# Moving one batch's q and k transposes from TensorE to the DMA queue in a fused attention and MLP kernel

## The chip, the cores and the metric

The kernel runs on one core of a Trainium2 chip. The metric is the device time of one execution in microseconds. Executions of one kernel on one chip mostly agree within 0.3%. "Fast" and "slow" are the states that each run was given: slow is a run more than 1.5% above the fastest of the same kernel.

## The reference, cut to what matters

```python
def _attn_ref(q, k, v):                      # 8 batches, 8 heads, 576 positions, 64 wide
    scores = np.matmul(q, k.transpose(0, 1, 3, 2)) / np.sqrt(D)
    mask = np.abs(pos[:, None] - pos[None, :]) <= 32
    ...softmax over the masked scores...
    return np.matmul(attn, v)

def _moe_ref(x, w_in, w_out):                # x: 4608 x 512, w_in: 512 x 2048
    h = x @ w_in
    g = np.where(h > 0.0, h, np.exp(np.minimum(h, 0.0)) - 1.0)
    return g @ w_out
```

A narrow band of attention feeds two large matrix products. The products are most of the work of TensorE; the attention is threaded between them.

## The kernel before

The loop has 144 steps. A step has eight matmuls `ps` (x times w_in), four `psY` (g times w_out, two steps behind), and in three places, "dve", "mid" and "end", whatever a table has put there: casts, transposes, scores, loads. A quiet step takes 1.735 us, eight steps with their attention 15.32 us.

```python
for kk in range(NSTEP + LAG):
    run(kk, "first")
    if 1 <= kk < NSTEP:
        elu(kk - 1)
    run(kk, "dve")
    if kk < NSTEP:
        mm1(kk)                  # ps
    run(kk, "mid")
    ...mm2(kk - LAG)...          # psY
    run(kk, "end")
```

Attention goes by pairs of blocks of 64 queries. Pair 9 is the first to need batch 2's q and k, pair 13 batch 3's (step 37), pair 18 batch 4's (step 58). Scores need q and k with the 64 channels on the partitions, so each batch's q and k are transposed, in one of two ways:

```python
# On TensorE (batches 0 to 2): cast, transpose against the identity, evict from PSUM
at(19 + n, "mid", cast_qk, b, which, WHOLE, j0, 9, nc.vector)
at(20 + n, "mid", transpose_qk, b, which, WHOLE, j0, 9, nc.scalar, "s")

# By DMA (batches 3 to 7): cast, write the rows to DRAM, transpose on the way back
def write_rows(b, which):                        # issued by ScalarE
    nc.scalar.dma_start(out=..., in_=qk_b.pop((b, which, 0))...)

def transpose_rows(b, which):                    # issued by SyncE's queue
    nc.sync.dma_start_transpose(
        out=keys_or_queries(b, which), in_=in_dram.pop((b, which)))

def x_dma(i):                                    # from pair 10 on; the same queue
    nc.sync.dma_start_transpose(out=xT_of(i), in_=x_st...)
```

The transpose waits for the rows to have landed. SyncE's queue also carries the loads of q and k, and the output. v is loaded by GpSimd in short rows; VectorE copies it from `Ve` to `Vo` a few steps later. A "gate" is a DMA of one element that waits for a tile: what stands behind it in the queue can't start earlier.

```python
for m in range(3, VS):
    load_v(1, m)                                                 # batch 1's last v
gate(w_out_sb[0:1, NFO // 4 - 1, D_MODEL - 1:D_MODEL])
for which in range(2):
    load_qk(1, which, HALF_A)
gate(w_in_at(3))                                                 # w_in's fourth quarter
for which in range(2):
    load_qk(1, which, HALF_B)
for which in range(2):
    load_qk(2, which, WHOLE)
```

The softmax here doesn't subtract the row's maximum and nothing guards it: scores larger than these inputs give would overflow.

## Time and profile before

| | before |
|---|---|
| median of 3 runs | 309.51 us (309.19 to 310.4) |
| span of the profiled run | 307.9 us |
| TensorE busy | 95% of the span |
| share of TensorE in the chain that ended last | 81% |

The lines of the profile that carry this are in the prediction below: TensorE is full from 31 us to the tail, so the steps can be followed by the starts of their `ps` groups. All step starts below are such starts in the profiled run, in us from the beginning of the span.

### The profile page before, as it was taken

Reading aid. Unit: us, or ns where it says so; the run is one execution under the profiler, and the core shown is the slowest. Engines: PE = TensorE matmul, PEld = TensorE weight load, DVE = VectorE, ACT = ScalarE, POOL = GpSimd, SP = SyncE. Lnnn points to the kernel's source line nnn. Section 1 sums busy time; section 2 is a strip of 40 time slices with the busy share of each in tenths; the row PEclk is TensorE's granted clock in tenths of the full one; section 3 lists DMA queues with packets and bytes.
Section 4 is the critical chain, followed back from the end, with each engine's and each line's share of the span. In section 5 each row is a group of like instructions: output and inputs, shape, how many; then the busy total and the mean of one; then the engine's idle time right before and its main releaser. Section 6 shows DMA issues by size and latency. Waiting matters only on the chain.

```text
span 307.9 us, 7525 instructions
## 1 busy us (share of the span) xinstructions
PE 291.5 (95%) x3009; PEld 196.9 (64%) x3062; DVE 245.8 (80%) x478; ACT 169.4 (55%) x254; POOL 45.8 (15%) x64
## 2 busy tenths in 40 slices
PE   6778999999999999999999999999999999999994
PEld 2546666676666666666666666666666666666662
DVE  6776688899978788888887888888888787876663
ACT  3635656787664674767376737673636363634331
POOL 8841100952220302020202010000000000000000
PEclk9799999999999999999999999999999999999999
DMA  9999999999999899799999998377111111111011
GB/s 188 190 193 273 188 257 387 302 191 223 293 166 195 289 255 206 170 165 331 156 140 197 322 261 183 111 178 159 70 36 68 36 70 35 70 34 70 0 70 68
DMA packets 91654, 52.33 MB, mean 170 GB/s; under 512 B 76516, under 2 KB 81124, under 8 KB 91620
## 3 DMA queue, kind: packets, MB, share of 16 engines
q1 hardware_dynamic: 47444, 35.60, 47.4%
q0 software_dynamic: 42304, 9.51, 40.1%
q10 hardware_dynamic: 1872, 6.75, 5.8%
q8 instruction: 24, 0.39, 0.5%
q14 instruction: 10, 0.08, 0.1%
HBM read 36.70 MB, written 15.34 MB: 169 GB/s over the span
## 4 chain that ended last, share of the span: by engine, by line
PE 81%; DVE 7%; DMA 4%; POOL 3%; issue 2%; ACT 1%; DVEq 0%; POOLq 0%
PE ps L582 38%; PE psY L616 36%; DMA w_in_sb<-in_moe_w_in_dram 4%; PE psS L328 3%; PE psS L296 3%; DVE g_sb L601 2%; POOL Ve L141 1%; PE ptx L271 1%; DVE m_sb L591 1%; DVE x_st L340 1%; DVE pm L316 1%; ACT e_sb L589 1%; POOL c L135 1%; DVE y_sb L228 1%; PE psXT L349 1%
## 5 line engine op out<-in xcount | busy, mean ns | idle before, releaser
L589 ACT ACTIVATE e_sb<-ps 128x512 f32<-128x512 f32 (+1 forms) x145 | 86.2, 595 | 123.0 <-PE ps L582 115.4
L582 PE MATMUL ps<-xT,w_in_sb 128*128 128x256 bf16 x1152 | 149.3, 273 | 2.7 <-DVE m_sb L591 0.9
L616 PE MATMUL psY<-w_out_sb,g_sb 128*128 128x512 bf16 x525 | 139.1, 379 | 4.2 <-DMA w_out_sb<-in_moe_w_out_dram 0.9
L582 PEld LDWEIGHTS <-w_in_sb 128*128 128x128 bf16 x1152 | 110.7, 98 | 41.0 <-issue 2.3
L601 DVE SCALAR_TENSOR_TENSOR g_sb<-ps,m_sb 128x512 bf16<-128x512 f32 (+1 forms) x145 | 99.5, 686 | 13.1 <-PE ps L582 0.5
L591 DVE TENSOR_SCALAR m_sb<-e_sb 128x512 bf16<-128x512 f32 (+1 forms) x145 | 62.2, 429 | 35.3 <-ACT e_sb L589 33.3
L616 PEld LDWEIGHTS <-g_sb 128*128 128x128 bf16 x576 | 54.5, 98 | 39.9 <-DVE g_sb L601 1.6
L141 POOL DMA_DIRECT2D Ve<-in_v_dram x40 | 35.0, 885 | 130.7 <-PE psS L328 93.6
L307 ACT ACTIVATE pu<-psS 128x1024 bf16<-128x1024 f32 x36 | 36.6, 1019 | 1.9 <-PE psS L296 1.9
L340 DVE TENSOR_TENSOR x_st<-psS,rc 128x512 bf16<-128x512 f32 x36 | 24.9, 692 | 2.3 <-DMA xT<-x_st 1.1
L316 DVE TENSOR_TENSOR pm<-pu,masks 128x1024 bf16<-128x1024 bf16 x36 | 24.6, 683 | 1.4 <-ACT pu L307 1.3
L226 ACT CAST qkb<-f 128x768 bf16<-128x768 f32 (+1 forms) x30 | 25.4, 848 | 0.0
L328 PEld LDWEIGHTS <-pm 128*64 128x64 bf16 x576 | 11.2, 110 | 9.7 <-DVE pm L316 6.7
L152 DVE COPY Vo<-Ve 64x1040 bf16<-64x1040 bf16 x32 | 13.8, 431 | 1.4 <-DMA Ve<-in_v_dram 0.4
L328 PE MATMUL psS<-Ve,pm 128*64 128x65 bf16 x320 | 13.8, 196 | 0.5 <-DVE pm L316 0.3
L296 PEld LDWEIGHTS <-kT 64*128 64x128 bf16 x576 | 10.0, 97 | 5.3 <-issue 4.2
L228 DVE COPY y_sb<-psY 128x512 f32<-128x512 f32 x18 | 12.3, 686 | 1.0 <-PE psY L616 0.9
L296 PE MATMUL psS<-qT,kT 64*128 64x64 bf16 x576 | 12.4, 193 | 0.5 <-DVE kT L228 0.5
L328 PE MATMUL psS<-Vo,pm 128*64 128x65 bf16 x256 | 12.4, 196 | 0.2 <-DVE pm L316 0.2
L226 ACT COPY y_sb<-psY 128x512 f32<-128x512 f32 x18 | 10.5, 583 | 2.2 <-PE psY L616 2.2
L226 ACT COPY qT<-ptx 128x1152 bf16<-128x1152 bf16 (+2 forms) x8 | 7.5, 971 | 3.1 <-PE ptx L271 2.4
L271 PE MATMUL ptx<-ident,qkb 128*128 128x128 bf16 x90 | 7.1, 223 | 2.0 <-DVE qkb L228 1.9
(35 smaller groups left out, 68.3 us busy)
## 6 DMA issues: line engine op xcount, KB each, us to landing
out_dram<-y_sb SPq DMA_DIRECT2D x35, 256.0 KB, 2.8
f<-in_q_dram SPq DMA_DIRECT2D x12, 576.0 KB, 8.4
f<-in_k_dram SPq DMA_DIRECT2D x12, 576.0 KB, 9.2
in_dram<-qkb ACTq DMA_DIRECT2D x10, 576.0 KB, 7.3
Ve<-in_v_dram POOLq DMA_DIRECT2D x24, 128.0 KB, 10.3
w_in_sb<-in_moe_w_in_dram POOLq DMA_DIRECT2D x4, 512.0 KB, 14.0
w_out_sb<-in_moe_w_out_dram POOLq DMA_DIRECT2D x4, 512.0 KB, 16.6
Ve<-in_v_dram POOLq DMA_DIRECT2D x16, 96.0 KB, 9.5
```

Of the source, the lines that this page charges most:

```text
L141: nc.gpsimd.dma_start(out=V_e[b % 3][p0:p1, m, :, 0:D], in_=v[b, :, lo + p0:lo + p1, :].rearrange("h p d -> p h d"))
L226: nc.scalar.copy(d_, s_)
L296: nc.tensor.matmul(psS[:, h % 2, hp * 128 + z * QB:hp * 128 + (z + 1) * QB], lhsT=kT[b % 2][base:base + 64, KPAD + hp * S + QB * qb - WIN: ...
L307: nc.scalar.activation(pu, _bap(psS, [psS.ap[0], [1, 1024]]), AX.Exp, scale=SCALE)
L316: nc.vector.tensor_mul(pm, pu, _bap(mm, [mm.ap[0], [0, H], [1, 2 * QB]]))
L328: nc.tensor.matmul(psS[QB * z:QB * (z + 1), par, hp * VD:(hp + 1) * VD], lhsT=pm[:, par * HP + hp, z * QB:(z + 1) * QB], rhs=vv[:, qb // 2 ...
L340: nc.vector.tensor_mul(x_st, _bap(psS, [psS.ap[0], [VD, HP], [512, 2], [1, D]]), _bap(rc, [rc.ap[0], [2, HP], [1, 2], [0, D]]))
L582: nc.tensor.matmul(ps[:, j, :], lhsT=w_in_sb[:, do, fo * 128:(fo + 1) * 128], rhs=xT[t][:, :, do, :], start=(do == 0), stop=(do == NDO - 1))
L589: nc.scalar.activation(e_sb, ps, AX.Exp)
L591: nc.vector.tensor_scalar(m_sb, e_sb, -1.0, None, ALU.add)
L601: nc.vector.scalar_tensor_tensor(g_t[kk][:, z * w:(z + 1) * w, :], ps, 0.0, m_t[kk][z], ALU.max, ALU.min)
L616: nc.tensor.matmul(psY[t][ts], lhsT=g_sb[:, j, ts * 128:(ts + 1) * 128], rhs=w_out_sb[:, s * FG + j, :], start=(s == 0 and j == 0), stop=( ...
```

## The change

The intent: take batch 2's 36 transposes (four groups of nine) off TensorE, which is the bound, and send its q and k the way of batches 3 to 7. To make room, batch 1's second half and batch 2 are loaded earlier (behind w_out's third quarter instead of w_in's fourth), batch 3's loads wait for batch 2's last cast of k, batch 4's come later, and pairs 8 to 11 begin two steps later. Cut to its core:

```diff
-    gate(w_in_at(3))
+    gate(w_out_sb[0:1, 3 * NFO // 4 - 1, D_MODEL - 1:D_MODEL])
     for which in range(2):
         load_qk(1, which, HALF_B)
-    for which in range(2):
+    for which in (1, 0):
         load_qk(2, which, WHOLE)
...          (batch 1's first cast of k: from step 8's "dve" to step 7's "end")
-    begin = {4: 9, 5: 12, 6: 17, 7: 19, 8: 25, 10: 30, 12: 37}
+    begin = {4: 9, 5: 12, 6: 17, 7: 19, 8: 27, 10: 32, 12: 37}
...          (pair 9's transpose of x on TensorE: from its step's "end" to "mid")
-        l_qk, l_v, c0 = {2: (0, 0, 0), 3: (15, 24, 22)}.get(
-            b, (max(k0 - 36, 24), k0 - 22, k0 - 22))
+        l_qk, l_v, c0 = {2: (0, 0, 0), 3: (18, 24, 22)}.get(
+            b, (k0 - 28, k0 - 22, k0 - 22))
+        if b == 3:
+            at(22, "dve", hold_v, 3)
...
         if b == 2:
-            for n, (which, j0) in enumerate(((0, 0), (0, 9), (1, 0), (1, 9))):
-                at(19 + n, "mid", cast_qk, b, which, WHOLE, j0, 9, nc.vector)
-                at(20 + n, "mid", transpose_qk, b, which, WHOLE, j0, 9,
-                   nc.scalar, "s")
-            continue
+            when = [(15, "end", nc.scalar), (16, "dve", nc.vector),
+                    (18, "mid", nc.scalar), (18, "end", nc.scalar),
+                    (20, "mid", nc.scalar), (20, "end", nc.scalar)]
...          (a gate on the last cast of k, at step 18)
+                at({18: 20, 20: 23}[kk] if b == 2 else
+                   kk + (3 if kk == 29 else 4), "mid",
                    transpose_rows, b, which)
```

`l_qk`, `l_v` and `c0` are the steps at which a batch's loads of q and k, its loads of v and its casts begin.

More of the change, by code (lines that the diff above doesn't have):

```diff
@@ L491 @@
         for which in range(2):
-            at(*((kq + which, "dve") if kq == 7 else (kq - 1 + which, "mid")),
-               cast_qk, 1, which, part, 0, SJ // 2,
+            at(*((kq, ("dve", "end")[which]) if kq == 7 else
+                 (kq - 1 + which, "mid")), cast_qk, 1, which, part, 0, SJ // 2,
                (nc.scalar, nc.vector)[which])
@@ L521 @@
         if i < FIRST_DMA:
-            at(n, "end", x_transpose, i)
-            at(n, "end", x_evac, i, nc.scalar)
+            slot = "mid" if i == FIRST_DMA - 1 else "end"
+            at(n, slot, x_transpose, i)
+            at(n, slot, x_evac, i, nc.scalar)
         else:
@@ L530 @@
         k0 = begin[first_pair(b)]
-        l_qk, l_v, c0 = {2: (0, 0, 0), 3: (15, 24, 22)}.get(
-            b, (max(k0 - 36, 24), k0 - 22, k0 - 22))
+        l_qk, l_v, c0 = {2: (0, 0, 0), 3: (18, 24, 22)}.get(
+            b, (k0 - 28, k0 - 22, k0 - 22))
+        if b == 3:
+            at(22, "dve", hold_v, 3)
         if b >= 3:
-            at(l_qk, "mid", load_qk, b, 0, WHOLE)
-            at(l_qk + 1, "mid", load_qk, b, 1, WHOLE)
+            at(l_qk, "end", load_qk, b, 0, WHOLE)
+            at(l_qk + (b > 3), "end", load_qk, b, 1, WHOLE)
             for m in range(VS):
                 at(l_v + m, "mid", load_v, b, m)
-        for n, back in enumerate((3, 2, 1, 0) if b == 2 else (10, 8, 3, 2)):
+        for n, back in enumerate({2: (3, 2, 1, 0), 3: (6, 5, 3, 2)}.get(
+                b, (10, 8, 3, 2))):
             m0 = 2 * (n // 2)
@@ L542 @@
         if b == 2:
-            for n, (which, j0) in enumerate(((0, 0), (0, 9), (1, 0), (1, 9))):
-                at(19 + n, "mid", cast_qk, b, which, WHOLE, j0, 9, nc.vector)
-                at(20 + n, "mid", transpose_qk, b, which, WHOLE, j0, 9,
-                   nc.scalar, "s")
-            continue
-        free = [f for f in range(c0, k0) if f not in starts]
-        for n, (which, j0) in enumerate(
-                (which, j0) for which in range(2) for j0 in (0, 6, 12)):
-            at(free[n], "end", cast_qk, b, which, WHOLE, j0, 6,
-               nc.vector if free[n] < 24 else nc.scalar)
-            if j0 == 12:
-                at(free[n], "end", write_rows, b, which)
-                at(free[n] + (3 if free[n] == 29 else 4), "mid",
+            when = [(15, "end", nc.scalar), (16, "dve", nc.vector),
+                    (18, "mid", nc.scalar), (18, "end", nc.scalar),
+                    (20, "mid", nc.scalar), (20, "end", nc.scalar)]
+        else:
+            when = [(f, "end", nc.vector if f < 24 else nc.scalar)
+                    for f in range(c0, k0) if f not in starts]
+        for n in range(6):
+            which, j0 = (n // 3 + (b == 2)) % 2, 6 * (n % 3)
+            kk, slot, eng = when[n]
+            at(kk, slot, cast_qk, b, which, WHOLE, j0, 6, eng)
+            if j0 == 12:
+                if b == 2 and which == 1:
+                    at(kk, slot, lambda: gate(
+                        qk_b[2, 1, 0][0:1, SJ - 1, 0:1]))
+                at(kk, slot, write_rows, b, which)
+                at({18: 20, 20: 23}[kk] if b == 2 else
+                   kk + (3 if kk == 29 else 4), "mid",
                    transpose_rows, b, which)
```

## The prediction

> **What bounds the kernel now.** I read the page from the top (busy shares, slices, the chain that ended last), then TensorE's timeline around the steps that change, then the DMA queue's timeline with landings.
>
> ```profile
> PE 291.5 (95%) x3009; PEld 196.9 (64%) x3062; DVE 245.8 (80%) x478; ACT 169.4 (55%) x254; POOL 45.8 (15%) x64
> ...
> PE   6778999999999999999999999999999999999994
> ...
> DMA  9999999999999899799999998377111111111011
> ...
> PE 81%; DVE 7%; DMA 4%; POOL 3%; issue 2%; ACT 1%; DVEq 0%; POOLq 0%
> ```
>
> The last instruction is reached through TensorE for 81% of the span, and from the fifth slice (31 us) on TensorE is busy over 90% until the tail. The chain says that work taken off TensorE shortens the kernel, and that work taken off ScalarE (55%) alone does not. The DMA row says that the 16 DMA engines are busy until about 200 us, so new transfers before that are not free.
>
> The loop has 144 steps of 8 matmuls into ps (line 582) and 4 into psY (line 616). Counting the ps groups dates the steps: step 8 starts at 33.80 us, 20 at 61.51, 27 at 77.19, 37 at 98.61. Batch 2's transposes (ptx) lie in steps 20 to 23. TensorE's timeline, with start, duration and operation (durations include a matmul's latency, so I use differences of starts):
>
> ```profile
> 33.80 1.04 PE L582 MATMUL ps<-xT,w_in_sb 128*128 128x256 bf16 x8
> 35.24 0.68 PE L271 MATMUL ptx<-ident,qkb 128*128 128x128 bf16 x9 [0.41 <-DVE qkb L228]
> ...
> 61.51 1.04 PE L582 MATMUL ps<-xT,w_in_sb 128*128 128x256 bf16 x8
> 62.39 0.67 PE L271 MATMUL ptx<-ident,qkb 128*128 128x128 bf16 x9
> 62.89 1.03 PE L616 MATMUL psY<-w_out_sb,g_sb 128*128 128x512 bf16 x4
> ...
> 99.57 0.76 PE L296 MATMUL psS<-qT,kT 64*128 64x64 bf16 x32
> ```
>
> The reader is to see three things: nine transposes take 62.89 - 62.39 = 0.50 us of TensorE's issue; in step 8 they came late, waiting for a cast on VectorE; and step 37's scores, the first with batch 3's keys, took 0.76 us, where the same group takes 0.64 elsewhere.
>
> Batch 3 already goes the way that batch 2 is to go. Its part of the queue timeline (the two transposes, and one of batch 5), then the landings, from the views of a tensor in a narrow window: batch 3's k rows into DRAM (issued at 85.63), its kT transpose (92.87), and batch 5's qT transpose (142.32):
>
> ```profile
> 82.60 5.56 SPq L257 DMA_TRANSPOSE qT<-in_dram  x1
> 92.87 3.54 SPq L257 DMA_TRANSPOSE kT<-in_dram  x1
> ...
> 142.32 9.73 SPq L257 DMA_TRANSPOSE qT<-in_dram  x1
> ...
> DMA to landing us min/median/max: 7.2/7.2/7.2
> ...
> DMA to landing us min/median/max: 7.1/7.1/7.1
> ...
> DMA to landing us min/median/max: 17.0/17.0/17.0
> ```
>
> So batch 3's k took 7.2 us to DRAM and 7.1 back: 92.87 + 7.1 = 99.97, just where step 37's long scores are. That route is already only just in time in the kernel before.
>
> **What the Trainium skill says.** "TensorE: Matmul & The Clock Gate", section "Wait — 56ns, not 53.3ns?": warm matmuls of 128 columns start 55.6 ns apart. The trace agrees: 0.50 us / 9 = 55.6 ns. "DMA: Bandwidth & Descriptors", section "Two DMAs through the same engine are not ordered": a DMA that reads what another wrote has to be issued after the first one's completion. The trace agrees: the kT transpose is issued at 92.87, when the rows have landed (85.63 + 7.2 = 92.8); the two latencies therefore add. The same page, section "Issuing engines are not separate DMA queues": all queues share the 16 engines. It agrees: the same 590 KB transpose lands after 4.6 us in the quiet at 207.7 us and after 17.0 at 142.3. "Advanced Engine Details and Errata", section "X-Bar Transpose (TRN2)", calls transpose DMAs as fast as ordinary ones; here only the quiet ones are near it (590 KB in 4.6 us is 128 GB/s, an ordinary q load of the same size lands in 4.2 to 12.5), so I take latencies from the trace.
>
> **The change, part by part.**
>
> 1. *Removed from TensorE:* 36 transposes of batch 2, 4 groups x 0.50 us = 2.0 us, all on the path. ScalarE loses four evictions of 1.28 us (timeline at 63.09, 65.82, 68.28, 70.52), VectorE four casts of 0.75. In their place six casts of 128x768: five on ScalarE at 0.82, one on VectorE at 0.55. ScalarE: -5.1 + 4.1; VectorE -3.0 + 0.55. ScalarE is off the path. VectorE is crowded just there (11.06 of 12 us between 63 and 75), but TensorE idles only 0.1 us of those 12, so its relief is worth at most some tenths.
> 2. *Batch 1's first k cast* moves from the head of step 8 (behind the elu of step 7) to the end of step 7. The transposes could start when step 8's ps matmuls are issued, 33.80 + 0.87 = 34.67, and started at 35.24. Gain 0.57 us, taken as 0.5.
> 3. *Added to the DMA queues:* two writes and two transposes of 590 KB. The gate now opens with w_out's third quarter, issued at 13.71 and landed 20.1 later, 33.8 us, instead of with w_in's fourth at 38.4. Batch 2's loads then start some 4 us earlier than 42 us and are there in time for step 15. Batch 3's loads wait for batch 2's last k cast (about 58.5 us), batch 3's v until step 22, batch 4's q and k until step 30 (before: 64 to 70 us).
> 4. *Moved:* scores, exponentials and masks of pairs 8 to 11 from steps 25 and 30 to 27 and 32. The work is the same. One new tight spot: pair 9's transpose now stands in the middle of step 31, and step 32's ps needs its eviction. Behind step 31's ps come ScalarE's exponential (0.60) and the eviction (0.59), 1.19 us, while TensorE has the transposes (0.23) and one psY group (0.87), 1.10. Cost 0.1 to 0.3 us.
>
> Removed: 2.0 + 0.5 = 2.5 us. With nothing given back the time is 309.5 - 2.5 = 307.0.
>
> **The rivals: what is given back.**
>
> *A. Step 27 waits for batch 2's qT.* The last q cast ends in step 20. Before, step 20's exponential ended at 63.19; less 0.5, plus two casts of 0.82, the write is issued at 64.3. Step 27's scores stood to start at 77.19 + 0.87 (its ps), less 2.5, less 0.58 for the scores of pairs 8 and 9 that no longer come before it: 75.0. The route has 10.7 us. The same route took, from write issue to transposed landing: batch 7's k 202.19 to 212.3 = 10.1; batch 4's k 117.89 to 128.65 = 10.8; batch 3's k 14.3; batch 5's q 134.94 to 159.3 = 24.4. The last had the next batch's loads around it, and batch 3's loads lie around batch 2's route now. For it: three of four are over 10.7 us. Against it: the change has been shaped for this, with k first, batch 3's v and batch 4's loads held out of the way, and the pairs moved two steps. A route of 14 us costs 3.3 us (time about 310.3), one of 20 costs 9 (316). I take no or a small stall as likeliest, and book 1.0 us on average.
>
> *B. VectorE waits for batch 3's q.* Its load is issued at about 59 us; the loads of this stretch landed in 8.4 to 11.5 us, so at 68 to 70. The first cast stands on VectorE at the end of step 22, about 67 us. VectorE runs in order, so step 22's elu waits behind it and then step 24's ps. Step 23 hides some 1.7 us. Expected 0.2 us, at worst 1.5.
>
> *C. Step 37 waits for batch 3's kT,* which had no slack. Its k chain is tied to steps 29 and 32, so it moves with TensorE, and steps 29 to 37 now hold about 1.1 us more TensorE work (pv of pairs 8 and 9, 0.68; their two transposes, 0.46). But batch 4's loads (2.36 MB) now run beside it. Expected 0.2 us, at worst 4.
>
> *D. A larger gain:* every small stall from step 9 to step 30 goes too. TensorE took 47.5 us for 21 steps of 1.735 (36.4) and about 8.7 of attention work and transposes; the rest, some 2.4 us, is stalls. Half of it gone, with no new wait, gives 305.8. There is nowhere a gain of 6 us.
>
> **Range and chances.** 307.0, plus 1.0 (A), 0.2 (B), 0.2 (C) and 0.1 (part 4) gives 308.5 us. The lower end is part 1 and 2 without any new wait and some stalls gone, 306.4; the upper end is A at about 16 us of route with a little of B or C, 313.0. Over 2% slower is over 315.7, a route near 20 us: 0.08. Over 2% faster is under 303.3, which only a gain larger than D could give: 0.02. Within 2%: 0.90.
>
> **What would show it.** No ptx groups after step 16, and steps 20 to 23 shorter by 0.50 us each: part 1. Step 8's ptx about 0.9 us behind its ps: part 2. A: an idle time of TensorE before psS in step 27, released by a DMA into qT. B: VectorE's cast in step 22 released by a DMA into f. C: the same as A in step 37. From step 40 on, a step should take what it took (15.32 us per 8 steps): any difference there would say that I misjudged what is moved. I would be wrong if qT lands several us after 75, or if the earlier gate slows w_in's or w_out's last quarter (needed near 43 and 48 us; landed at 38.4 and 41.7), a wait I have counted as nothing.

## The result, and the profile after

| | before | after |
|---|---|---|
| median (4 runs each, same chip) | 309.95 us (309.19 to 311.98) | 329.35 us (328.54 to 331.27) |
| span of the profiled run | 307.9 us | 329.3 us |
| mean granted clock of that run | 0.994 | 0.966 |

The ratio is 1.0624, 95% interval 1.0554 to 1.0694: slower. A ratio here is the mean time of one kernel's fast runs over that of the other's in the same rounds, so it is not quite the ratio of the medians.

The page of the kernel after. Each digit is a fortieth of the span, 8.23 us; PE is TensorE's busy share in tenths, PEclk its granted clock, DMA the busy share of the DMA engines:

```profile
PE 297.4 (90%) x3026; PEld 197.1 (60%) x3026; DVE 245.2 (74%) x476; ACT 168.3 (51%) x255; POOL 45.5 (14%) x64
...
PE   7678995998029899999999999999999999999994
...
PEclk9999997999658999999999999999999999999998
DMA  9999993999999996999999969939522120211011
...
PE 72%; DMA 22%; DVE 2%; POOL 2%; ACT 1%; issue 1%; POOLq 0%; DVEq 0%
```

TensorE has two holes: a small one in the seventh slice (49 to 58 us) and a deep one in the eleventh and twelfth (82 to 99 us). The clock falls with both. From there on the row is as before. DMA has gone from 4% to 22% of the chain that ended last: TensorE is no longer the only bound.

Step starts show where the 21 us of these two runs came from:

| stretch | before, us | after, us | difference |
|---|---|---|---|
| step 8 begins | 33.80 | 34.93 | +1.13 |
| 8 to 14 | 13.72 | 13.14 | -0.58 |
| 14 to 20 | 13.99 | 18.90 | +4.91 |
| 20 to 24 | 9.67 | 7.86 | -1.81 |
| 24 to 27 | 6.01 | 6.58 | +0.57 |
| 27 to 28 | 2.51 | 17.44 | +14.93 |
| 28 to 40 | 25.65 | 27.96 | +2.31 |
| 40 to 143 | 194.85 | 194.56 | -0.29 |

The gains are there: 0.58 us in step 8 and 1.81 in steps 20 to 23. Two stretches swallow them. Of the 2.31 us after step 28, 0.87 is a slow clock in step 28 itself (3.28 us instead of 2.41), and about 1.14 is work of pairs 8 and 9 that came before step 28 in the kernel before (see e13). The 1.13 us at the head is no effect of the change: experiment e4, with the same front, begins step 8 at 33.71.

**The first hole.** TensorE's timeline in steps 14 to 16 (start, duration, operation; in brackets the idle time before it and what ended it): the same wait in the kernel before, then the kernel after, then VectorE's line there that ended it:

```profile
49.59 0.40 PE L349 MATMUL psXT<-ident,x_st 128*128 128x128 bf16 x4 [0.16 <-DVE x_st L340]
...
48.07 1.05 PE L590 MATMUL ps<-xT,w_in_sb 128*128 128x256 bf16 x8
48.95 1.03 PE L624 MATMUL psY<-w_out_sb,g_sb 128*128 128x512 bf16 x4
53.46 0.40 PE L349 MATMUL psXT<-ident,x_st 128*128 128x128 bf16 x4 [3.48 <-DVE x_st L340]
53.69 1.43 PE L590 MATMUL ps<-xT,w_in_sb 128*128 128x256 bf16 x8
54.92 1.16 PE L271 MATMUL ptx<-ident,qkb 128*128 128x128 bf16 x9
55.88 1.88 PE L624 MATMUL psY<-w_out_sb,g_sb 128*128 128x512 bf16 x4
57.58 1.05 PE L590 MATMUL ps<-xT,w_in_sb 128*128 128x256 bf16 x8
```

```profile
52.13 0.43 DVE L152 COPY Vo<-Ve 64x1040 bf16<-64x1040 bf16 x1 [3.35 <-DMA Ve<-in_v_dram]
```

TensorE waited for VectorE (x_st), but VectorE had waited for v. The last two loads of batch 1's v went out at 27.0 and 31.2 us before and at 26.9 and 31.6 after. Their landings, before:

```profile
DMA to landing us min/median/max: 16.0/16.0/16.0
DMA to landing us min/median/max: 12.4/12.4/12.4
```

and after:

```profile
DMA to landing us min/median/max: 25.2/25.2/25.2
DMA to landing us min/median/max: 20.9/20.9/20.9
```

So v came 9 us later from loads issued at the same time. What is new between 34 and 43 us is the eight loads of q and k behind the gate, issued at 34.9 to 39.4 instead of from 39.1 on. The packets of the kernel after show what became of v meanwhile: queue q0 is GpSimd's, with v in packets of 126 bytes on average, q1 SyncE's, with the loads. First 46 to 50 us, then 50 to 52 (packets, MB, share of the 16 engines):

```profile
q1 hardware_dynamic: 345, 1.41, 92.4%
q0 software_dynamic: 470, 0.06, 22.8%
...
q0 software_dynamic: 849, 0.11, 87.6%
q1 hardware_dynamic: 29, 0.09, 13.1%
```

While the loads ran, v got 118 packets per us, and 425 once they were through. The hole costs more than its 3.48 us: the next three groups (`ps`, `ptx`, `psY`) take 57.58 - 53.69 = 3.89 us where they take 0.87 + 0.50 + 0.87 = 2.24 at full clock, another 1.65. The Trainium skill, "TensorE: Matmul & The Clock Gate", section "What's actually happening", says that TensorE's clock is halved after an idle window of about 3.4 us. The trace agrees here: a `psY` group shows 1.88 us and 1.03 elsewhere. But waits of 2.05 to 2.45 us were enough in e5 and e12, while waits of 2.19 to 2.66 us in e3, e7 and e11 left the clock at full speed, so the length of one wait does not decide it; the measurements come before the figure.

**The second hole.** TensorE in step 27, kernel after. The first 16 matmuls of psS are pair 8's (batch 1), the next 16 pair 9's (batch 2):

```profile
81.41 1.05 PE L590 MATMUL ps<-xT,w_in_sb 128*128 128x256 bf16 x8
82.39 0.41 PE L296 MATMUL psS<-qT,kT 64*128 64x64 bf16 x16
96.62 0.61 PE L296 MATMUL psS<-qT,kT 64*128 64x64 bf16 x16 [13.83 <-DMA qT<-in_dram]
97.16 1.89 PE L624 MATMUL psY<-w_out_sb,g_sb 128*128 128x512 bf16 x4
98.84 1.91 PE L590 MATMUL ps<-xT,w_in_sb 128*128 128x256 bf16 x8
100.55 1.73 PE L624 MATMUL psY<-w_out_sb,g_sb 128*128 128x512 bf16 x4
102.12 1.04 PE L590 MATMUL ps<-xT,w_in_sb 128*128 128x256 bf16 x8
```

A wait of 13.83 us for batch 2's qT; then three groups at half clock, 102.12 - 97.16 = 4.96 us instead of 3 x 0.87, another 2.35. The queues of ScalarE (row writes) and SyncE (gates, loads, transposes) show the route; each line is an issue, its duration the time the issuing took:

```profile
64.44 0.63 ACTq L252 DMA_DIRECT2D in_dram<-qkb  x1
...
70.12 0.59 ACTq L252 DMA_DIRECT2D in_dram<-qkb  x1
```

```profile
64.44 0.65 SPq L163 DMA_DIRECT2D gate<-qkb  x1
65.14 1.90 SPq L123 DMA_DIRECT2D f<-in_q_dram  x2
67.08 1.27 SPq L123 DMA_DIRECT2D f<-in_k_dram  x2
69.99 9.25 SPq L257 DMA_TRANSPOSE kT<-in_dram  x1
83.06 6.66 SPq L257 DMA_TRANSPOSE qT<-in_dram  x1
```

The landings after the issue: k's rows, k's transpose, q's transpose.

```profile
DMA to landing us min/median/max: 5.5/5.5/5.5
...
DMA to landing us min/median/max: 18.4/18.4/18.4
...
DMA to landing us min/median/max: 13.5/13.5/13.5
```

k's transpose was issued at 69.99, behind batch 3's four loads in the same queue, took 9.25 us to issue and landed at 88.4. q's rows went out at 70.12; their transpose, which has to wait for them, was issued 12.9 us later, although the queue had been free since 79.2, and landed at 96.6. The route of q took 96.58 - 70.12 = 26.5 us. TensorE was ready for it at 96.62 - 13.83 = 82.8, so 12.7 us were to be had.

### The profile page after: what moved, and what is told of

Its sections match the earlier page's. It is cut to its first block, busy times and chain, and to the rows that moved or that the text cites. A ratio compares the mean times of both kernels' runs of the same rounds, so it can differ in the third digit from the quotient of the medians.

```text
span 329.3 us, 7510 instructions
## 1 busy us (share of the span) xinstructions
PE 297.4 (90%) x3026; PEld 197.1 (60%) x3026; DVE 245.2 (74%) x476; ACT 168.3 (51%) x255; POOL 45.5 (14%) x64
## 4 chain that ended last, share of the span: by engine, by line
PE 72%; DMA 22%; DVE 2%; POOL 2%; ACT 1%; issue 1%; POOLq 0%; DVEq 0%
PE psY L624 33%; PE ps L590 32%; DMA Ve<-in_v_dram 10%; DMA w_out_sb<-in_moe_w_out_dram 4%; DMA qT<-in_dram 4%; DMA in_dram<-qkb 4%; PE psS L328 3%; PE psS L296 3%; POOL Ve L141 1%; ACT qkb L226 0%; PE ptx L271 0%; DVE x_st L340 0%; DVE g_sb L609 0%; ACT e_sb L597 0%; ACT y_sb L226 0%
## 5 line engine op out<-in xcount | busy, mean ns | idle before, releaser
L624 PE MATMUL psY<-w_out_sb,g_sb 128*128 128x512 bf16 x576 | 150.1, 384 | 2.2 <-DVE y_sb L228 0.8
L624 PEld LDWEIGHTS <-g_sb 128*128 128x128 bf16 x576 | 55.2, 99 | 42.6 <-issue 3.4
L226 ACT CAST qkb<-f 128x768 bf16<-128x768 f32 (+1 forms) x35 | 29.5, 846 | 0.8 <-ACT qkb L226 0.8
L296 PE MATMUL psS<-qT,kT 64*128 64x64 bf16 x576 | 12.5, 194 | 14.3 <-DMA qT<-in_dram 13.8
L152 DVE COPY Vo<-Ve 64x1040 bf16<-64x1040 bf16 x32 | 14.7, 459 | 5.6 <-DMA Ve<-in_v_dram 4.7
L328 PE MATMUL psS<-Vo,pm 128*64 128x65 bf16 x256 | 12.2, 196 | 0.7 <-DVE Vo L152 0.5
L226 ACT COPY xT<-psXT 128x512 bf16<-128x512 bf16 x10 | 5.9, 586 | 5.0 <-PE psXT L349 5.0
L349 PE MATMUL psXT<-ident,x_st 128*128 128x128 bf16 x40 | 3.9, 220 | 4.6 <-DVE x_st L340 4.6
```

The source lines that it names most:

```text
L226: nc.scalar.copy(d_, s_)
L296: nc.tensor.matmul(psS[:, h % 2, hp * 128 + z * QB:hp * 128 + (z + 1) * QB], lhsT=kT[b % 2][base:base + 64, KPAD + hp * S + QB * qb - WIN: ...
L328: nc.tensor.matmul(psS[QB * z:QB * (z + 1), par, hp * VD:(hp + 1) * VD], lhsT=pm[:, par * HP + hp, z * QB:(z + 1) * QB], rhs=vv[:, qb // 2 ...
L624: nc.tensor.matmul(psY[t][ts], lhsT=g_sb[:, j, ts * 128:(ts + 1) * 128], rhs=w_out_sb[:, s * FG + j, :], start=(s == 0 and j == 0), stop=( ...
```

## The experiments

The theory after the result: the TensorE savings are real, and two transfers come late, v because of the gate and batch 2's q and k because the route shares queue and engines with batch 3's loads and v. The rivals: that the route is too long whatever lies around it; that the DMA engines have no room for it before about 110 us, so that a wait turns up wherever one is taken away. Each was run in 3 rounds (e1 to e7) or 5 (e8 to e14) beside the kernel before, whose medians were 309.29 to 310.13. One run each of e3, e10, e12 and e13 (328.73, 324.26, 318.34 and 314.49 us) was slow and is in no ratio.

**e1: the change with the gate put back.**

```diff
-    gate(w_out_sb[0:1, 3 * NFO // 4 - 1, D_MODEL - 1:D_MODEL])
+    gate(w_in_at(3))
```

> The changed kernel with the gate for batch 1's second half and batch 2 put back on w_in's fourth quarter. Theory: the 3.5 us wait in step 14 is for batch 1's last v rows, which the earlier loads crowd out (25.2 and 20.9 us to land instead of 16.0 and 12.4); with the gate back they land in 16 and 12 again, the wait in step 14 is under 0.5 us, steps 15 and 16 run at full clock, and the time falls by about 5 us to 324 (323 to 325). The wait for qT in step 27 stays at 12 to 15 us. Rival: v is late for another reason (the order of the loads or the DMA state of the run); then 328 to 331, and the wait in step 14 stays.

Measured: 323.04 us, ratio 1.0447 (1.0405 to 1.0489). Step 14 takes 2.30 us, as before, and the two loads of v land after 16.2 and 12.2 us again. Step 27 still waits 11.87 us for qT. So the gate made the first hole, and the second has another cause.

**e2: the kernel before with the gate of the change, nothing else.** (The edit of e1 the other way round, in the kernel before.)

> The kernel before with that gate alone moved to w_out's third quarter, everything else as it was. Theory: the same v rows come late and step 14 waits 3 to 4 us, and the clock falls behind it: 309.5 + 5 = 314 to 316. Rival: without the rest of the change the earlier loads are harmless: 309 to 310.5.

Measured: 316.97 us, 1.0241 (1.0207 to 1.0275), somewhat more than expected. TensorE and VectorE in step 14:

```profile
56.52 0.61 PE L349 MATMUL psXT<-ident,x_st 128*128 128x128 bf16 x4 [6.77 <-DVE x_st L340]
```

```profile
55.19 0.43 DVE L152 COPY Vo<-Ve 64x1040 bf16<-64x1040 bf16 x1 [6.65 <-DMA Ve<-in_v_dram]
```

The two loads of v landed after 27.8 and 27.3 us. The gate alone, which adds and removes no byte, costs over 7 us. With e1 it settles the first hole. That it costs more here than in the change may come from batch 3's four loads, which follow at once (40.3 to 45.7 us) where the change holds them back; this was not tested.

**e3: the change with batch 3's v held seven steps longer** (and its copies accordingly later).

```diff
-3: (18, 24, 22)    at(22, "dve", hold_v, 3)    3: (6, 5, 3, 2)
+3: (18, 29, 22)    at(29, "dve", hold_v, 3)    3: (4, 3, 2, 1)
```

> The changed kernel with batch 3's v held until step 29, behind the scores that wait for qT (its copies to the odd blocks two steps later). Theory: these loads take the DMA engines from batch 2's qT transpose, which landed after 13.5 us; without them it lands after 7 to 9, and the time falls by 4 to 6 us to 323 to 325. Rival: the transposes are slow by themselves or held up in their own queue; then qT's landing stays at 12 to 14 us and the time at 328 to 331.

Measured: 324.96 us, 1.0483 (1.0428 to 1.0537). The wait in step 27 falls from 13.83 to 4.24 us: q's route now takes 15.8 us, since its transpose is issued at 78.61 and lands in 7.1. So v was a large part of the second hole. Some of it is given back in step 37, where batch 3's kT is now waited for 2.65 us: its transpose took 14.3 us to land beside the v that had been moved there, and 5.0 in the change.

**e4: the change with q's transpose ahead of k's in the queue.**

```diff
-                at({18: 20, 20: 23}[kk] if b == 2 else
+                at({18: 23, 20: 22}[kk] if b == 2 else
```

> The changed kernel with the two transposes of batch 2 queued in the other order: q first, so that neither starts before q's rows are written. Theory: q's row write took 12.9 us because k's transpose was in flight beside it (k's own took 5.5); alone it lands in 5 to 7, both transposes are through by about 90 instead of 96.6, and the time falls by 5 to 8 us to 321 to 324. Rival: what slows the write is batch 3's loads and v, not k's transpose; then the write still takes 10 us or more, the two transposes come behind it one after the other, and the time stays at 328 or rises to 335.

Measured: 329.91 us, 1.0664 (1.0599 to 1.0728): no gain, a miss. q's rows had landed by 77.8 where in the change they took until 83, as the theory had it, but then k's transpose, issued at 83.92, landed 11.2 us later beside v, and step 27 waited 12.18 us for kT. Step 27 needs both, so their order is worth nothing.

**e5: e1 with batch 3's loads back at step 15**, as before the change, ahead of batch 2's row writes.

```diff
-3: (18, 24, 22)
+3: (15, 24, 22)
```

> The changed kernel with the gate back on w_in's fourth quarter (which alone gave 323.0), and batch 3's q and k loads queued at step 15 behind batch 2's, as before the change, instead of behind batch 2's last k cast. Theory: in the run with the gate back these 2.36 MB stood in the queue ahead of k's transpose and beside both row writes; without them k's transpose starts when its rows land, q's rows land in 5 to 7 us and qT 4 to 6 us earlier: the wait in step 27 falls from 11.9 to 6 to 8 us and the time to 317 to 319. Rival: batch 3's v alone holds the transposes up; then the wait and the time stay within 1.5 us of that run.

Measured: 316.8, 317.24 and 316.95 us, all slow because a fourth run took 310.92; so there is no ratio. In the profiled run (316.8 us) k's transpose takes 2.49 us to issue instead of 9.25, q's route 14.9 us, and step 27 waits 2.45 us. This agrees with e3 on what the route suffers from, but rests on a run of the slow state. All four runs of e5 (310.92 to 317.24) do lie below all four of e1 (322.5 to 324.76), from which only batch 3's loads differ, though they ran on another chip.

**e6: e5 with batch 3's v held to step 27.**

```diff
-3: (15, 24, 22)    at(22, "dve", hold_v, 3)    3: (6, 5, 3, 2)
+3: (15, 27, 22)    at(27, "dve", hold_v, 3)    3: (4, 3, 2, 1)
```

> The same, and batch 3's v held until step 27 as well. Theory: with both out of the way the route takes its quiet time, 9 to 11 us from the write to qT: the wait in step 27 is 0 to 2 us and the time 308 to 311, unless the v that is now later makes a wait of its own near step 37 (up to 3 us, 313). Rival: the transposes are slow by themselves beside the row writes; then at least 5 us of wait stay and the time is over 314.

Measured: 315.67 us, 1.0168 (1.0125 to 1.0211). The second hole is gone, and step 37 has a new one. TensorE:

```profile
75.39 0.41 PE L296 MATMUL psS<-qT,kT 64*128 64x64 bf16 x16 [0.29 <-DMA qT<-in_dram]
...
103.79 0.40 PE L296 MATMUL psS<-qT,kT 64*128 64x64 bf16 x8 [5.05 <-DMA kT<-in_dram]
```

So the route isn't too long in itself: q took 63.86 to 75.3, 11.5 us. But v now goes out where batch 3's k has to pass: its transpose is issued at 88.99 and takes 14.8 us to land (13.0 in e10, where v lies there too and batch 4's loads come only at its end). Batch 4's loads have a part in the wait as well: they were issued at 77.87 to 79.79, and batch 3's k rows beside them took 8.2 us to DRAM, in e10 4.4. e9 moves them away. The wait has moved ten steps on.

**e7: e1 with batch 2 back on TensorE**, all else of the change kept, to weigh the route by itself.

```diff
         if b == 2:
-            when = [(15, "end", nc.scalar), (16, "dve", nc.vector), ...
+            for n, (which, j0) in enumerate(((0, 0), (0, 9), (1, 0), (1, 9))):
+                at(19 + n, "mid", cast_qk, b, which, WHOLE, j0, 9, nc.vector)
+                at(20 + n, "mid", transpose_qk, b, which, WHOLE, j0, 9, nc.scalar, "s")
+            continue
```

> The changed kernel with the gate back and batch 2's q and k transposed on TensorE again; everything else of the change stays (pairs 8 to 11 two steps later, the cast of batch 1, batch 3's loads and v later). Theory: the route is the whole rest of the loss, so this is as fast as before: 309 to 310.5, with no wait over 1 us in steps 27 or 37. Rival: the two steps' shift or the later loads cost something themselves, in the steps that the long wait hides: 312 or more.

Measured: 310.85 us, 1.001 (0.996 to 1.0059). Without the route the rest of the change, gate apart, costs nothing that can be told, though step 37 waits 2.19 us for kT. Beside e1 that puts 12 us on the route as the change has it. e6 begins step 27 at 73.71 where e7 begins it at 76.67, 3 us ahead; but batch 3's loads and v differ too, so this is not the route alone (e9 and e10 give 2.3 us, e13 and e14 2.05), and the later wait takes all of it.

**e8: the kernel before with batch 1's first cast of k moved, alone.**

```diff
-            at(*((kq + which, "dve") if kq == 7 else (kq - 1 + which, "mid")),
-               cast_qk, 1, which, part, 0, SJ // 2,
+            at(*((kq, ("dve", "end")[which]) if kq == 7 else
+                 (kq - 1 + which, "mid")), cast_qk, 1, which, part, 0, SJ // 2,
```

> The kernel before with the cast of batch 1's first k half alone moved to the end of step 7. The changed kernel gained 0.58 us from step 8 to 9 (2.24 instead of 2.82). Theory: the gain stays to the end: 0.4 to 0.6 us, ratio 0.998. Rival: it is taken back at the next wait on VectorE or a DMA before step 16: ratio 1.000.

Measured: 309.4 us, 0.9971 (0.9925 to 1.0017): inconclusive. The interval holds both the 0.5 us of the theory and nothing. One execution, the profiled one, took 606.62 us with every step twice as long, for no reason that the profile shows; it was left aside.

**e9: e6 with batch 3's last casts up to step 27 (rows out two steps earlier) and batch 4's loads at step 34.**

```diff
-3: (15, 27, 22)}
+3: (15, 27, 22), 4: (34, 36, 40)}
-                    for f in range(c0, k0) if f not in starts]
+                    for f in range(c0, k0) if f not in starts or b == 3]
```

> The run with the gate back, batch 3's loads early and its v at step 27 (315.7), with two more moves: batch 3's last k cast in step 27 instead of 29, so that its rows are written two steps earlier, and batch 4's q and k loads from step 30 to 34, behind batch 3's kT transpose in the queue. Theory: that run had no wait left in step 27 and was 3 us ahead of the one on TensorE there; all of its loss stood in step 37, where it waited 5 to 6 us for batch 3's kT, which is the same route one batch later. With both moves that wait is under 1 us and the time is 306.5 to 309, ratio 0.990 to 0.997: faster than before by what was taken off TensorE. Rival: the DMA engines have no room for the route anywhere before 100 us, and the wait turns up again in step 37 or at batch 4 (step 58): 311 or more.

Measured: 319.43 us, 1.0325 (1.0273 to 1.0377). Neither step 27 nor step 37 waits any more, and step 37 begins 1.24 us ahead of the kernel before. Then:

```profile
108.62 1.65 PE L591 MATMUL ps<-xT,w_in_sb 128*128 128x256 bf16 x7 [4.42 <-DMA xT<-x_st]
...
148.82 0.64 PE L296 MATMUL psS<-qT,kT 64*128 64x64 bf16 x32 [3.43 <-DMA kT<-in_dram]
```

The first is step 40: x of pairs 10 and 11 is transposed by the queue that now holds batch 4's loads; the second of the two was issued at 98.26, behind the last of the loads at 97.55. The Trainium skill, "DMA: Bandwidth & Descriptors", section "Queues, rings and completion order", says that an engine takes the descriptors of a ring in order; the wait agrees with that, though sharing the engines would make one too. The second is step 58: batch 4's k is late because everything of batch 4 was moved back.

**e10: e9 with batch 2 on TensorE** (the edit of e7).

> The same schedule with batch 2's q and k transposed on TensorE. Theory: no wait in steps 27 and 37 either, so it differs from the run beside it by the 2.0 us of the transposes and some tenths of stalls: 308.5 to 310, that is 1.5 to 3 us slower than the route. Rival: the schedule, not the route, makes the gain: then both have the same time within 0.7 us.

Measured: 321.46 us, 1.0341 (1.0283 to 1.0399). The same waits at 40 and 58, without the route. They belong to the places of batch 4's loads, not to the route's bytes. Step 27 begins at 76.51, in e9 at 74.23: the route is worth 2.3 us there.

**e11: e9 with batch 4's loads at steps 31 and 32**, right behind batch 3's transpose of k, ahead of those of x, and its casts from step 36.

```diff
-4: (34, 36, 40)
+4: (31, 36, 36)
```

> The kernel of e9 with batch 4's q and k loads at steps 31 and 32, so in the queue right behind batch 3's transpose of k and ahead of the transposes of x for pairs 10 and 11, and its casts from step 36. Theory: e9 had no wait left in steps 27 and 37 and was 1.2 us ahead of the kernel before at step 37; it lost 4.4 us in step 40, where the transpose of x for a pair stood behind batch 4's loads in the same queue, and some 5 us at step 58, where batch 4's k came late. With the loads ahead of those transposes both waits go: 307.5 to 309, ratio 0.992 to 0.999. Rival: there is no room for the route anywhere, and the wait turns up again in step 37 (the loads share the engines with batch 3's transpose), 36, 40 or 58: 311 or more.

Measured: 313.26 us, 1.0136 (1.0109 to 1.0163): better than e9 by 6 us, but the theory's 309 was missed. The wait in step 58 is gone, and step 37 begins at 97.30, 1.31 us ahead of the kernel before. Steps 37 to 40 lose it. ScalarE:

```profile
100.81 0.83 ACT L226 CAST qkb<-f 128x768 bf16<-128x768 f32 x1 [3.63 <-DMA f<-in_q_dram]
```

and TensorE:

```profile
103.45 1.03 PE L591 MATMUL ps<-xT,w_in_sb 128*128 128x256 bf16 x8 [1.71 <-DVE g_sb L610]
...
108.89 1.03 PE L591 MATMUL ps<-xT,w_in_sb 128*128 128x256 bf16 x8 [2.66 <-DMA xT<-x_st]
```

The cast had been put where its load had not landed, and the exponential that stands behind it on ScalarE ran only after it, at 101.55; x still came late. From step 40 to 143 the kernel takes 194.5 us, as before: nothing else is wrong with it.

**e12: e11 with pairs 8 to 11 one step earlier** (26 and 31) and pair 9's transpose back at its step's end.

```diff
-8: 27, 10: 32        slot = "mid" if i == FIRST_DMA - 1 else "end"
+8: 26, 10: 31        slot = "end"
```

> The kernel of e11 with pairs 8 to 11 beginning at steps 26 and 31 in place of 27 and 32 and pair 9's transpose back at its step's end. Theory: in e9 the transpose of x in step 31 waited about 1.05 us for its source rows, because pair 9's work came close behind pair 8's; batch 2's q was through at about 73 us where 72.9 is needed. The wait in 31 goes and none comes in 26: 306.5 to 308. Rival: step 26 now waits for the transpose of q, up to 2 us, and nothing is gained over e11.

Measured: 315.7 us, 1.0185 (1.0148 to 1.0222): a miss. The wait of step 31 went (0.73 us of it came back in step 29) and none came in 26, but step 37 begins at 97.35, no sooner than in e11 (VectorE's g_sb held up the two steps before it by 0.38 and 0.66 us), and the waits before the `ps` of steps 39 and 40 are still there, 2.38 and 2.05 us. Behind each the granted clock was 0.50 for 3.4 us, where e11 shows 1.00 after its 1.71 and 2.66 us: from step 38 to 41 this kernel took 13.36 us and e11 10.79.

**e13: e11 with x of pairs 10 and 11 transposed on TensorE, and batch 4's casts from step 38.** This and e14 were run to settle what e9 to e12 left open: only transfers too close to their users, or want of room.

```diff
-    FIRST_TWO, FIRST_DMA, BACK_AT = 8, 10, 18
+    FIRST_TWO, FIRST_DMA, BACK_AT = 8, 12, 18
-            slot = "mid" if i == FIRST_DMA - 1 else "end"
+            slot = "mid" if i == 9 else "end"
-4: (31, 36, 36)
+4: (31, 36, 38)
```

> The kernel of e11 with the transposes of x for pairs 10 and 11 on TensorE (two groups of 0.23 us and two evictions on ScalarE of 0.59) in place of the DMA queue, and batch 4's casts two steps later (from step 38). e11 was 1.3 us ahead of the kernel before at step 37 and lost 4.9 us up to step 40: ScalarE's first cast of batch 4 waited 3.6 us for its load, TensorE 2.7 us for the transposed x; from step 40 on its steps took what they took before. Theory (transfers placed too close to their users, no want of room): both waits go, 0.5 us of the lead is paid for the two transposes: 308 to 309.5, ratio 0.995 to 1.000. Rival (no room for the route before 110 us): a wait of 2 us or more turns up in step 36 to 42 on v or on a load, or in step 58: 311 or more.

Measured: 309.54 us against 309.75, ratio 0.9986 (0.9958 to 1.0014), just at the upper end of what the theory said. Two small transposes of x (131 KB each) are off the queue in it. From step 14 to step 60 TensorE waits for a DMA only once, 0.26 us for kT in step 58. The queue of batch 2's transposes and TensorE in step 27:

```profile
66.37 2.74 SPq L257 DMA_TRANSPOSE kT<-in_dram  x1
69.20 2.21 SPq L257 DMA_TRANSPOSE qT<-in_dram  x1
```

```profile
74.01 1.05 PE L591 MATMUL ps<-xT,w_in_sb 128*128 128x256 bf16 x8
74.99 0.64 PE L296 MATMUL psS<-qT,kT 64*128 64x64 bf16 x32
75.56 1.04 PE L625 MATMUL psY<-w_out_sb,g_sb 128*128 128x512 bf16 x4
```

The lines to hold beside them are those of the kernel after: there the issuing took 9.25 and 6.66 us and the second half of psS came 13.83 us late. Here q's rows left at 64.16, its transpose was issued at 69.20 and landed 4.8 us later: a route of 9.8 us instead of 26.5, and one microsecond to spare. Step 28 begins at 76.43, 3.27 us ahead of the kernel before. Of that 1.14 is work only put off (the pv of pairs 8 and 9, 0.68, and their transposes, 0.46), the rest is gain. Up to step 37 the lead falls to 0.38: the work put off, 0.46 for two more transposes of x, and small waits. Those of TensorE in steps 28 to 36 (0.50 us for VectorE's pm, 1.04 and 0.42 for its x_st, 0.34 for ScalarE's y_sb) sum to 2.30 us where those of the kernel before in the same steps sum to 1.0.

**e14: e13 with batch 2 on TensorE** (the edit of e7).

> The kernel of e13 with batch 2's q and k back on TensorE, all else equal. Theory: the route is worth the 2 us of TensorE's transposes as long as nobody waits for it, so this is 1.5 to 2.5 us slower than e13. Rival (no room): without the route's two writes and two transposes on the DMA engines the transfers of batch 3 and 4 land earlier, and this is as fast as e13 or faster.

Measured: 311.0 us, 1.0037 (1.0016 to 1.0058). Both ratios are against the same runs of the kernel before: 0.9986 / 1.0037 = 0.995, so the route is worth 0.5%, 1.5 us of the medians. The schedule that makes room for it costs nearly as much by itself: without the route it is 1.25 us above the kernel before. The theory's range is met at its edge; the rival, no slower than e13, is out.

## Why the prediction was wrong

- **The bound** was named rightly for the kernel before. The prediction also said that the DMA engines are busy until 200 us and that new transfers "are not free". It then priced them by latencies from other places.
- **Part 1, the transposes removed:** right. Steps 20 to 23 lost 1.81 us in the kernel after against 2.0 predicted, and e13 beside e14 keeps 1.5 of it to the end.
- **Part 2, the cast:** right in the trace (0.58 us in step 8 against 0.5). By the clock it could not be told (e8).
- **Part 3, the gate:** wrong. The prediction saw the loads some 4 us earlier only as a gain, and named w_in's and w_out's last quarters as what might suffer, "a wait I have counted as nothing". What suffered was batch 1's v, which was not named at all. It cost 4.91 us between steps 14 and 20 (e1 and e2 show the gate as the cause). This term was 0 in the sum.
- **Part 4, the tight spot of pair 9:** the step was right, the wait and its size not. Predicted were 0.1 to 0.3 us in which step 32's ps waits for ScalarE's eviction; no such wait shows in the kernel after, in e1 or in e13. What TensorE waited for was VectorE's x_st, before the transposes of step 31: 0.83 us in the kernel after, 0.82 in e1, 1.04 in e13.
- **Rival A is the step that failed.** The mechanism, the place and the releaser are as predicted: psS in step 27, released by a DMA into qT. The size is not. "I take no or a small stall as likeliest, and book 1.0 us on average" stands against 13.83 us of wait and 2.35 us of slow clock after it. The available time was judged well, 10.7 us against 12.7 here and 10.8 in e13. The term that was mis-sized is the route: 26.5 us. The list of four routes held one of 24.4 us, with the next batch's loads around it, and the prediction itself said that batch 3's loads lie around batch 2's route. It then trusted that "the change has been shaped for this". The list was also a kind sample: the same trace has four more routes with both landings, of 13.9 (batch 7's q), 16.9 and 21.0 (batch 6's k and q) and 21.9 us (batch 5's k). Six of the eight were 13.9 us or longer. e3 and e6, and with the reserve made there e5, show what filled the route: batch 3's v and batch 3's loads. Cleared of both it took 9.8 us (e13), like the best of the list.
- **The slow clock** after a long wait was in no term. It added 1.65 and 2.35 us.
- **Rival B:** right, at most tenths: VectorE's cast waited 0.32 us for batch 3's q (at 73.61). Its other waits for a load of q or k lie in the first 7 us. Its like came in e11 and e12 on ScalarE, for batch 4's load.
- **Rival C:** "had no slack" was right. The kernel after doesn't show it, since TensorE was late itself; as soon as TensorE was earlier, step 37 waited 2.19 (e7) to 5.05 us (e6). The 0.2 us booked were too few.
- **The check on steps 40 to 143** holds: 194.56 us against 194.85.

What is settled: both holes are waits for transfers placed too close to their users, and the savings are real once nobody waits (e13 and e14). That the engines lacked room is out as a general cause, since e13 sends the same two writes and two transposes through without a wait in step 27 and with 0.26 us later, though with two small transposes of x fewer. That the loads of q and k slowed v's packets is seen in the packet counts (118 per us beside them, 425 after), and the effect of the gate is shown by e1 and e2; the rule by which the engines share between queues was not tested. No version beat the kernel before by more than the noise.

## What to carry to other kernels

A step moved from the bound engine to a transfer is worth its engine time only if the latency, taken under the traffic that will be there and summed over every dependent hop, is shorter than the slack; list every comparable case in the trace, not a few, and take those with the same traffic around them as the likely ones. Before issuing a load earlier, list every transfer in flight at that time and ask for each when it is needed, for the one that loses need not be in the same queue. When a wait is taken away, look at the next user of the same queue before running: here it moved from step 27 to 37, 38, 40 and 58.

## What the Trainium skill lacked or had wrong

- "Advanced Engine Details and Errata", section "X-Bar Transpose (TRN2)", has transposes as fast as ordinary DMAs, and gives no time for one in traffic. The same transpose of 590 KB landed in 4.8 us (e13), in 13.5 and in 18.4 us (the kernel after). Ordinary transfers of that size slowed as well, from 4.2 us for a load of q to 12.5 for one of k in the kernel before (the prediction calls the 12.5 a q load; the slowest q load with a recorded landing took 10.6), so the runs do not show the page wrong.
- "TensorE: Matmul & The Clock Gate", section "What's actually happening", has an idle window of about 3.4 us before the clock is halved. In e5 and e12 the granted clock fell to 0.50 for 3.4 us after waits of 2.45, 2.09, 2.38 and 2.05 us; after waits of 2.65 (e3), 2.66 (e11) and 2.19 us (e7) it stayed at 1.00.
- No page gives a time for what loads on SyncE's queue cost the short rows that GpSimd loads: batch 1's v landed after 25.2 and 20.9 us instead of 16.0 and 12.4 once eight loads of q and k were issued 4 us sooner, and after 27.8 and 27.3 us in e2, where the gate is the only edit.
